# Emitting the magnitude, clamp and low word of the next weight piece one step earlier in the float64 conversion of a fused attention and expert kernel

## The chip, the cores and the metric

One NeuronCore of a Trainium2 chip runs the whole program. The metric is the device time of one execution in microseconds (us). Five engines work side by side, each through its own queue in order: TensorE (PE; PEld is its weight load), VectorE (DVE), ScalarE (ACT), GpSimd (POOL) and SyncE (SP), which issues most DMAs.

## The reference, cut to what matters

Decayed linear attention over 4 batches, 8 heads, 768 positions of 64 values gives x (3072 by 512). A capacity router gives each of 8 experts 384 tokens, and each expert applies a two-layer network to its tokens. All tokens then pass through a shared second network:

```python
    for e in range(E):
        mask = assigned == e
        h = np.maximum(x[mask] @ w1[e], 0.0)
        out[mask] = h @ w2[e]
...
    h = x @ w_in
    g = np.maximum(h, 0.0) + np.log1p(np.exp(-np.abs(h)))
    return (g @ w_out).astype(np.float32)
```

The two weights w_in (512 by 2048) and w_out (2048 by 512) reach the chip as 64-bit floats, and the kernel turns them into 32-bit floats itself.

## The kernel before, in words

**Stages.** Attention runs over 24 chunks of 128 rows (class `Attn`). The first phase of the router picks expert and tokens for the first network (class `Route`). Then the experts run one after the other (class `Ffn`), while the router's next phase is issued piece by piece between their groups of matmuls. Every fp32 product is made of three matmuls: each operand is split into a rounded high part and the rest (`whi` and `wlo`, `gh` and `gl`, `xh` and `xl`, `x2h` and `x2l`), and high times high, low times high and high times low are added up in PSUM.

**The conversion** (class `Conv`, lines 240 to 318). A piece is a tile `raw` with two 32-bit words per weight. `load` (L254) brings it by a DMA on SP. `size` (L266 to L273) makes three instructions: ScalarE takes the magnitude of the high word (Abs, L270, into `cA`), GpSimd clamps it from below in place (the maximum, L271), and ScalarE scales the low word (L272, into `cB`). Then VectorE merges the sign into `cB` (the merge, L285), VectorE shifts `cA` (the shift, L287), and GpSimd adds `cA` and `cB` (the addition, L288). In the conversion of w_in a rounded copy on ScalarE (L298) and its rest on VectorE (L293, L301) follow.

`run` is a generator and each `yield` ends one step. A piece has two steps when it has one target (w_out), and mostly three when it has two (w_in). `size` is called for a later piece, `lead` pieces ahead.

The class is used twice:

- w_in: 16 pieces of 128 by 512 during attention, `lead` 2, five buffers of `cA` and four of `cB`. Its steps are spread over the 72 places that `Attn.emit` offers by `side(j, part)`, from the tenth place on.
- w_out: 32 pieces of 128 by 256 during the first router phase and expert 0 (the late conversion), `lead` 1, three buffers of `raw` and `cA`, two of `cB`. The buffers are taken in turn, so `cB` of piece q is the buffer of piece q-2, which the addition of piece q-2 reads.

**The order of expert 0.** `Ffn.plan` writes out a list of groups of matmuls, and `Ffn.emit` goes through it. For each group it first splits the weights that will be needed some groups later (`weights`, L661 on ScalarE and L662 on VectorE), then issues the group, then the conversion's steps, then a part of the router:

```python
            self.weights(at[n] + 4)
            fn(i, f)
            if i == 0 and n > 3:
                for _ in range(1 + n % 2):
                    self.late.step()
            step += 1
            if self.listed <= i + 1 or step % 2 == 0:
                self.route()
```

So an even group takes one step and an odd group two, until the pieces are done. The first groups of expert 0 are its own network (`m1`, L684 to L687 with h1h and h1l; `m2`, L676 to L678). From n = 18 on a group of w_in (`f1`, matmuls at L684 to L687, even n) and a group of w_out (`f2`, L782 to L787, odd n) alternate, until groups that transpose expert 1's rows (`xt`, L708, with xh and xl at L671 and L672) come between. In a w_in group ScalarE makes `gh` of the group before (L761) and three activations `sp` (L744 to L746), VectorE makes `gl` (L762) and `gf` (L748). `gh` and `gl` of group f are used by the w_out group f, which comes behind the w_in group f+2.

The router's operations on VectorE that matter here are `thr` (L476), `ind` (L487), `tb` (L540) and the one-hot `ohq` (L567). Their small matmuls on TensorE (L436, L490, L543, L580) stand between the large groups. The tokens' rows of expert 1 are gathered by three DMAs on GpSimd's queue (L697).

Of the kernel before, what the change touches and what calls it, by code (L numbers as in the profile page):

```python
# [244 lines left out]
class Conv:  # L245
# [29 lines left out]
    def run(self):  # L275
        nc, v, N = self.nc, self.nc.vector, len(self.plan)
        self.ahead(0)
        ready = [self.size(q) for q in range(self.lead)]
        late = None
        for p in range(N):  # L280
            self.ahead(p + 1)
            A, B, w1 = ready.pop(0)
            to = self.plan[p][1]
            F = to[0].bitcast(I32) if len(to) == 1 else A
            v.scalar_tensor_tensor(B, w1, UPPER, B, op0=OP.bitwise_and, op1=OP.bitwise_or)  # L285
            yield
            v.tensor_scalar(A, A, 3, 0x3fffffff, op0=OP.logical_shift_left, op1=OP.bitwise_and)  # L287
            nc.gpsimd.tensor_tensor(F, A, B, op=OP.add)  # L288
            if p + self.lead < N:
                ready.append(self.size(p + self.lead))  # L290
            yield
            if late:
                v.tensor_tensor(late[1][1], late[0], late[1][0].bitcast(FT), op=OP.subtract)  # L293
                yield
            late = None
            if len(to) == 2:
                late = F.bitcast(FT).rearrange("p (a n) -> p a n", a=4), to
                nc.scalar.activation(to[0], late[0], AF.Copy)  # L298
            self.made += 1
        if late:  # L300
            v.tensor_tensor(late[1][1], late[0], late[1][0].bitcast(FT), op=OP.subtract)  # L301
        while True:
            yield self
# [703 lines left out]
```

## Time and profile before

| | |
|---|---|
| median of 3 runs | 1018.38 us (1016.86 to 1020.95) |
| profiled execution | 1018.63 us, of which the span of instructions is 1016.9 us |
| mean granted TensorE clock over the span | 0.99 |
| TensorE (PE) busy | 994.5 us, 98% |
| VectorE (DVE) busy | 637.5 us, 63% |
| ScalarE (ACT) busy | 579.9 us, 57% |
| GpSimd (POOL) busy | 160.2 us, 16% |
| loads of w_in pieces, of w_out pieces, issue to landing | 8.7 us, 3.0 us (median) |

Attention ends at about 110 us, the first router phase at about 145 us, and the late conversion's last addition starts at 252 us. A busy TensorE is not TensorE at its peak, since the ends of pipelined matmuls are modelled. A wait is put down to the instruction that released it last. Averages over the whole span say little here: the conversion lives in the first quarter.

### The profile page before, as it was taken

How to read it: one execution, taken by the hardware profiler on the slowest of the kernel's cores; microseconds unless marked ns; L12 is line 12 of the kernel's file. 1: busy time of each engine (PE TensorE's matmuls, PEld its weight loads, DVE VectorE, ACT ScalarE, POOL GpSimd, SP SyncE). 2: the span in 40 equal slices, each digit the busy share in tenths (PEclk: the TensorE clock that was granted, in tenths of full speed). 3: DMA queues.
4: the chain of work that ended last, by engine and by line, in shares of the span. 5: the costliest groups of instructions: out<-in, count | busy, mean ns of one | idle time of the engine just before them, and what ended most of it. 6: DMA issues, size and time to landing. Idle time of an engine off the chain costs nothing.

```text
span 1016.9 us, 19118 instructions
## 1 busy us (share of the span) xinstructions
PE 994.5 (98%) x7319; PEld 899.3 (88%) x7319; DVE 637.5 (63%) x1620; ACT 579.9 (57%) x1250; POOL 160.2 (16%) x185
## 2 busy tenths in 40 slices
PE   9999889999999999999999999999999999999997
PEld 8888669887998889998998899899989999999996
DVE  6989678879666656755575566555665644444442
ACT  5999425777446653665456635654366536653663
POOL 1655223556101010100110010001010010000001
PEclk9999789999999999999999999999999999999999
DMA  9998234224412023200410031103210250013000
GB/s 367 414 415 357 95 115 159 87 71 121 119 39 63 2 68 100 61 1 25 143 57 7 22 125 53 32 11 105 63 32 4 80 166 1 1 57 111 1 1 31
DMA packets 40603, 96.05 MB, mean 94 GB/s; under 512 B 5312, under 2 KB 5568, under 8 KB 40512
## 3 DMA queue, kind: packets, MB, share of 16 engines
q1 hardware_dynamic: 36528, 82.16, 23.9%
q0 software_dynamic: 3840, 12.59, 3.7%
q8 instruction: 57, 0.93, 0.4%
q14 instruction: 34, 0.28, 0.1%
q10 hardware_dynamic: 144, 0.09, 0.0%
HBM read 82.23 MB, written 12.58 MB: 93 GB/s over the span
## 4 chain that ended last, share of the span: by engine, by line
PE 75%; issue 12%; POOL 4%; DVE 4%; ACT 3%; DMA 1%; another core or an unknown queue 0%; POOLq 0%; ACTq 0%
PE h L684 11%; PE h L687 11%; PE h L685 10%; PE acc L782 7%; PE acc L783 7%; PE acc L787 7%; PE acc L676 3%; PE acc L678 3%; PE acc L677 3%; PE pA L130 2%; PE pY L158 2%; PE pX L183 2%; PE rt L436 2%; POOL wol L288 1%; POOL cA L271 1%
## 5 line engine op out<-in xcount | busy, mean ns | idle before, releaser
L748 DVE SCALAR_TENSOR_TENSOR gf<-h,sp 128x384 f32<-128x384 f32 x128 | 71.2, 556 | 186.7 <-ACT sp L746 186.7
L684 PE MATMUL h<-x2h,wih 128*128 128x384 f32 x512 | 175.6, 343 | 1.5 <-DVE xl L672 1.5
L685 PE MATMUL h<-x2h,wil 128*128 128x384 f32 x512 | 172.5, 337 | 0.0
L782 PE MATMUL acc<-whi,gh 128*128 128x512 f32 x384 | 153.3, 399 | 0.0
L783 PE MATMUL acc<-wlo,gh 128*128 128x512 f32 x384 | 151.3, 394 | 0.0
L744 ACT ACTIVATE sp<-h 128x384 f32<-128x384 f32 x128 | 62.4, 487 | 135.6 <-PE h L687 125.3
L668 ACT ACTIVATE h1h<-h 128x384 fp32r<-128x384 f32 x64 | 31.4, 491 | 147.2 <-PE h L687 105.1
L687 PE MATMUL h<-x2l,wih 128*128 128x384 f32 x512 | 112.2, 339 | 0.9 <-DVE x2l L672 0.8
L787 PE MATMUL acc<-whi,gl 128*128 128x512 f32 x384 | 111.2, 396 | 0.8 <-DVE gl L762 0.8
L795 POOL DMA_INDIRECT out_dram<-rows,ix x24 | 24.2, 1007 | 500.0 <-ACT rows L793 496.6
L684 PEld LDWEIGHTS h<-x2h,wih 128*128 128x128 f32 x512 | 96.2, 188 | 5.2 <-DVE xl L672 1.8
L685 PEld LDWEIGHTS h<-x2h,wil 128*128 128x128 f32 x512 | 96.2, 188 | 3.4
L687 PEld LDWEIGHTS h<-x2l,wih 128*128 128x128 f32 x512 | 91.3, 188 | 3.1 <-DVE x2l L672 3.1
L662 DVE TENSOR_TENSOR wlo<-wraw,whi 128x512 fp32r<-128x512 f32 x128 | 86.6, 691 | 6.5 <-ACT whi L661 6.4
L662 DVE TENSOR_TENSOR wlo<-wol,whi 128x512 fp32r<-128x512 f32 x128 | 88.9, 698 | 0.9 <-ACT whi L661 0.9
L684 PE MATMUL h<-xh,whi 128*128 128x384 f32 x256 | 88.2, 345 | 0.7 <-ACT xh L671 0.7
L787 PEld LDWEIGHTS acc<-whi,gl 128*128 128x128 f32 x384 | 72.0, 188 | 18.6 <-DVE gl L762 1.4
L676 PE MATMUL acc<-h1h,whi 128*128 128x384 f32 x256 | 88.4, 345 | 0.0
L661 ACT ACTIVATE whi<-wraw 128x512 fp32r<-128x512 f32 x128 | 76.6, 624 | 17.3 <-DMA wraw<-in_moe_w_dram 16.0
L678 PE MATMUL acc<-h1l,whi 128*128 128x384 f32 x256 | 86.1, 336 | 0.0
L685 PE MATMUL h<-xh,wlo 128*128 128x384 f32 x256 | 86.1, 336 | 0.0
L677 PE MATMUL acc<-h1h,wlo 128*128 128x384 f32 x256 | 86.1, 336 | 0.0
(199 smaller groups left out, 1902.7 us busy)
## 6 DMA issues: line engine op xcount, KB each, us to landing
wraw<-in_moe_w_dram SPq DMA_DIRECT2D x128, 256.0 KB, 2.6
qk_t<-in_qk_dram SPq DMA_DIRECT2D x24, 512.0 KB, 8.6
kv_t<-in_kv_dram SPq DMA_DIRECT2D x24, 512.0 KB, 9.0
raw<-in_moe_w_in_dram SPq DMA_DIRECT2D x16, 512.0 KB, 8.7
raw<-in_moe_w_out_dram SPq DMA_DIRECT2D x32, 256.0 KB, 3.0
xd<-xs SPq DMA_DIRECT2D x24, 256.0 KB, 4.9
rows<-xd,ix POOLq DMA_INDIRECT x24
out_dram<-rows,ix POOLq DMA_INDIRECT x24
```

The lines of the kernel that those rows point to most:

```text
L661: nc.scalar.activation(hi, raw, AF.Copy)
L662: nc.vector.tensor_tensor(lo, raw, hi.bitcast(FT), op=OP.subtract)
L676: nc.tensor.matmul(ps, wh, ah, start=start, stop=False)
L677: nc.tensor.matmul(ps, wl, ah, start=False, stop=False)
L678: nc.tensor.matmul(ps, wh, al, start=False, stop=stop)
L684: mm(ps, wh(d), ah[:, d], start=d == 0, stop=False)
L685: mm(ps, wl(d), ah[:, d], start=False, stop=False)
L687: mm(ps, wh(d), al[:, d], start=False, stop=d == 3)
L748: nc.vector.scalar_tensor_tensor(g, ps, 0.0, a, op0=OP.max, op1=OP.add)
L782: nc.tensor.matmul(ps, gh[:, s], wh, start=f == 0, stop=False)
L783: nc.tensor.matmul(ps, gh[:, s], wl, start=False, stop=False)
L787: nc.tensor.matmul(ps, gl[:, s], wh, start=False, stop=f == 15)
```

## The change

In `Conv.run`, the call of `size` for the piece `lead` ahead moves from the end of a piece's second step to the end of its first step. In program order it stood behind the shift and the addition of the present piece; now it stands ahead of them and behind the merge.

```diff
             v.scalar_tensor_tensor(B, w1, UPPER, B, op0=OP.bitwise_and, op1=OP.bitwise_or)
+            if p + self.lead < N:
+                ready.append(self.size(p + self.lead))
             yield
             v.tensor_scalar(A, A, 3, 0x3fffffff, op0=OP.logical_shift_left, op1=OP.bitwise_and)
             nc.gpsimd.tensor_tensor(F, A, B, op=OP.add)
-            if p + self.lead < N:
-                ready.append(self.size(p + self.lead))
             yield
```

Both conversions are changed by it, since both are this class.

## Rows read from the trace of the kernel before

**Rows 1.** Busy time by stage: us, PE, PEld, DVE, ACT, POOL, PEclk, DMA, GB/s
```profile
22.00:44.00 22.00, 21.62 (x342) 18.50 (x344) 18.44 (x40) 21.90 (x67) 15.27 (x10) 1.00 1.03 415
147.00:185.00 38.00, 37.13 (x295) 35.76 (x295) 30.07 (x77) 20.31 (x45) 13.92 (x15) 1.00 0.43 132
185.00:253.00 68.00, 63.52 (x389) 55.84 (x388) 57.88 (x158) 50.20 (x114) 40.50 (x44) 1.00 0.31 94
```

**Rows 2.** Waits of PE from 145 to 255 us: total us, times, longest
```profile
PE h L684 <- DVE xl L672: 1.5, 1, 1.5
PE rt L490 <- DVE ind L487: 1.4, 1, 1.4
...
PE acc L787 <- DVE gl L762: 0.8, 1, 0.8
PE rt L543 <- DVE tb L540: 0.8, 1, 0.8
```

**Rows 3.** Waits of DVE from 145 to 255 us
```profile
DVE cA L287 <- POOL cA L271: 7.4, 8, 1.4
```

**Rows 4.** Timeline of POOL, the late conversion's additions: start us, us, instruction, idle before
```profile
193.48 0.84 POOL L288 TENSOR_TENSOR wol<-cA,cB 128x256 int32<-128x256 int32 x1 [4.70 <-DVE cA L287]
...
196.13 0.74 POOL L288 TENSOR_TENSOR wol<-cA,cB 128x256 int32<-128x256 int32 x1 [0.68 <-DVE ksat L493]
...
201.23 0.84 POOL L288 TENSOR_TENSOR wol<-cA,cB 128x256 int32<-128x256 int32 x1 [0.73 <-DVE cA L287]
...
205.88 0.84 POOL L288 TENSOR_TENSOR wol<-cA,cB 128x256 int32<-128x256 int32 x1 [2.99 <-DVE cA L287]
...
211.87 0.85 POOL L288 TENSOR_TENSOR wol<-cA,cB 128x256 int32<-128x256 int32 x1 [2.38 <-DVE cA L287]
...
223.71 1.92 POOL L288 TENSOR_TENSOR wol<-cA,cB 128x256 int32<-128x256 int32 x1 [5.33 <-DVE cA L287]
...
231.96 0.85 POOL L288 TENSOR_TENSOR wol<-cA,cB 128x256 int32<-128x256 int32 x1 [1.05 <-DVE cA L287]
...
242.57 0.83 POOL L288 TENSOR_TENSOR wol<-cA,cB 128x256 int32<-128x256 int32 x1 [0.64 <-ACT whi L661]
```

**Rows 5.** Timeline of ACT, low words of the late conversion
```profile
192.84 0.41 ACT L272 ACTIVATE cB<-raw 128x256 int32<-128x256 uint32 x1
...
200.17 0.43 ACT L272 ACTIVATE cB<-raw 128x256 int32<-128x256 uint32 x1
...
206.75 0.43 ACT L272 ACTIVATE cB<-raw 128x256 int32<-128x256 uint32 x1 [0.77 <-POOL wol L288]
...
209.84 0.42 ACT L272 ACTIVATE cB<-raw 128x256 int32<-128x256 uint32 x1
...
219.11 0.42 ACT L272 ACTIVATE cB<-raw 128x256 int32<-128x256 uint32 x1
...
230.82 0.41 ACT L272 ACTIVATE cB<-raw 128x256 int32<-128x256 uint32 x1
...
241.59 0.42 ACT L272 ACTIVATE cB<-raw 128x256 int32<-128x256 uint32 x1
```

**Rows 6.** Waits of ACT from 194 to 243 us
```profile
ACT cB L272 <- POOL wol L288: 8.0, 6, 3.0
ACT sp L744 <- PE h L687: 2.3, 2, 1.9
ACT gh L761 <- DVE gf L748: 1.7, 1, 1.7
ACT cA L270 <- DMA raw<-in_moe_w_out_dram: 1.0, 2, 0.8
ACT sp L744 <- PE rt L537: 0.6, 1, 0.6
```

**Rows 7.** Timeline of DVE, the router's thresholds
```profile
196.15 0.77 DVE L476 SCALAR_TENSOR_TENSOR thr<-ksat,jio 128x32 f16<-128x32 f32 x1
...
261.97 0.21 DVE L476 SCALAR_TENSOR_TENSOR thr<-ksat,jio 128x46 f16<-128x46 f32 x1
```

## The prediction

> **What bounds the kernel now.** I read the stages first, then the waits of each engine in the stage where the change can act, then the single instructions there. TensorE is busy nearly the whole span (the table above), so a change off TensorE is worth only what it takes from, or adds to, TensorE's idle time. [Rows 1] give the three stages in which the conversion runs: in attention ScalarE is as full as TensorE (21.90 of 22 us, DMA share 1.03); in the first matmuls of expert 0 (147 to 185 us) TensorE has 37.13 of 38 us; in the long stage after it (185 to 253 us) TensorE has 63.52 of 68 us, so 4.5 us are open there, and VectorE (57.88) and ScalarE (50.20) are both loaded. [Rows 2] name what TensorE waits for: xl 1.5, ind 1.4, gl 0.8 and tb 0.8 us, each made by VectorE in its queue's order. That queue in turn waits 7.4 us in 8 places for the conversion's maximum on GpSimd [rows 3]. So the end is set by TensorE, and in this stage by a ring of ScalarE, VectorE and GpSimd that is nearly as slow.
>
> **What moves.** Per piece three instructions are issued one step earlier: Abs on ScalarE, maximum on GpSimd, low word on ScalarE. Nothing is added or removed; no DMA moves, because the loads are issued at the head of each piece as before, and SP's queue keeps its order. On GpSimd maximum p+1 now stands ahead of addition p. On VectorE nothing changes place.
>
> What matters is a reuse, not the order itself. In the late conversion cB has two buffers, so the low word of piece q may be written only when addition q-2 has read its buffer. Before, low word p+1 stood two steps behind addition p-1; now it stands one step behind. Expert 0's groups take one step (a w_in group, L684 to L687) and two steps (a w_out group, L782 to L787) in turn, so three pieces make a period of four groups. I call the w_out group that holds the second step of p and the first of p+1 **split**, and the one that holds both steps of p+2 **whole**.
>
> **Whole groups.** Before, ScalarE runs two pieces back to back behind the three sp activations and stops at the second low word until the addition of the group before: it starts at 206.75 [rows 5], when the addition of 205.88 ends [rows 4]. After, one of the two has gone forward, but the other stops for the same addition, at the same instant. Cost 0. VectorE gains: maximum p+2 is long done when the shift asks for it, so most of the 7.4 us go.
>
> **Split groups.** Before, one piece, no wait. After, that piece stands in the w_in group ahead, and the next follows at once: Abs runs, then the low word waits for addition p, which stands behind gf, the merge, routing work and the shift of this same group on VectorE. Behind that low word are queued, on ScalarE, the next whi, gh and sp, and for these wait wlo, gl, gf and the routing chain on VectorE. From the rows: the low word of 200.17 ends at 200.60 and frees ScalarE; after the change a low word of 0.43 us follows the end of the addition of 201.23, 202.07, and ScalarE is free at 202.50: 1.9 us later. In the same way, low word against addition [rows 4, 5]: 192.84 against 193.48 1.5 us, 209.84 against 211.87 2.9, 219.11 against 223.71 6.5, 230.82 against 231.96 2.0, 241.59 against 242.57 1.8. Of the 6.5 I take 4.5: that addition lasted 1.92 us where 0.84 is usual, and VectorE should come to its shift about a microsecond earlier. Sum 14.6 us.
>
> **What takes it up.** ScalarE's own idle time between them: for TensorE 2.3 and 0.6, for gf 1.7, for a load 1.0 [rows 6], and 3.0, the longest wait for an addition in [rows 6], held there by the gather of rows on GpSimd and not by the conversion's order. That is 8.6 us, which leaves 6.0. VectorE's saved waits shorten the split group of 209.84 by one wait, 1.4 us at the most [rows 3]: 4.6 us.
>
> **The port.** An operation of VectorE that meets one of GpSimd ends with it: thr takes 0.77 us from 196.15 [rows 7], and the addition of 196.13 lasts 0.74 [rows 4]; the same line takes 0.21 us at 261.97 with GpSimd free [rows 7]. After the change maximum p+1 starts just ahead of each split group, while the merge of p is due on VectorE, and addition p hangs on the shift behind that merge. It costs between nothing (the merge comes first) and a whole operation of GpSimd, 0.84 us as an addition [rows 4]. I take 0.3 in each of six places, nearer the low end, because the maximum must itself wait for Abs while gf and the merge are already next in VectorE's queue: 1.8 us. The Trainium skill ("SBUF — State Buffer", section "SBUF: two separate sides") states the rule: the pair of ports that VectorE and GpSimd share is an exclusive lock, and "the other fully blocks". The trace agrees (0.77 against 0.21 us). By the rule alone each of the six would pay the whole operation; that is a rival below.
>
> **Sum.** 4.6 and 1.8 make 6.4 us by which ScalarE is late at the end of the stage. TensorE pays it only where it has no reserve: at ind, tb, gl and xl it waits already [rows 2], and the last of them, xl, comes behind all six places; between them gh is made about two groups ahead of its use. I take two thirds, 4.3 us. Ends: nothing if the reserve takes it all, 8 us if none does and the port costs more; below nothing, the waits of TensorE that hang on VectorE alone, xl 1.5, gl 0.8 and tb 0.8, could go, minus 3.1.
>
> **Costed at nothing.** Attention: cB has four buffers there and the addition asked for is three steps back, so no new wait. The first step now holds three pieces' activations instead of two ahead of sb and vh, but ScalarE is full from 22 to 44 us [rows 1] and does the same work by the end of that stretch; bounds 1.2 us (one piece) either way. Loads: each waits for a merge that keeps its place, but Abs asks for it one step earlier; ScalarE waits 1.0 us in two places for loads now [rows 6], and where the load is later still, the low word behind it waits for its addition anyway, so I add nothing (at most another 1.0). Routing ahead of expert 0: the shifts and additions keep their order on VectorE, and GpSimd waits for them. First matmuls of expert 0: ScalarE is busy 20.31 of 38 us [rows 1], which covers the same waits; without that cover they would cost about as much as three split groups, some 5 us.
>
> The profiled execution took 1018.63 us, the median of the runs is 1018.38. 1018.63 and 4.3 make 1022.9; against the median I say 1022.7.
>
> **Rivals.** (a) *As forecast*, +2 to +7, likeliest 1022.7. For it: [rows 4, 5] fix each wait. Chance 0.45. (b) *The port decides*: the merge or shift waits a whole 0.84 us in each split group, 0.54 us more six times, 3.2: about 1025.9. It decides if Abs ends well ahead of gf in most groups. Against it: ScalarE finishes sp, for which gf waits, just ahead of Abs, so gf starts while Abs runs. Chance 0.20. The skill's rule of the exclusive lock, named above, speaks for this one. (c) *Hidden*: gh and wlo stand far enough ahead, TensorE waits as before: 1018.4. For it: ScalarE waits 8.0 us for additions already [rows 6], and TensorE's four waits come to 4.5 us [rows 2]. Chance 0.25. (d) *Faster*: the 7.4 us that VectorE waits for the maximum [rows 3] were what made xl, gl and tb late. Without them TensorE gains up to 3.1 us: 1015.3. It decides if those three waits shrink while the low words wait no longer than 8 us in that window; against it, xl needs xh, which stands on ScalarE behind the low word. Chance 0.10.
>
> **How the numbers follow.** 0.5% (5.1 us) is about what a measurement of this kernel can tell from no change. Slower by more: four tenths of (a) and nearly all of (b), 0.38. Faster by more: a corner of (d), 0.05. The rest, 0.57, is within. The range takes in (c) and most of (b), and reaches into (d): 1016.0 to 1028.5; the likeliest case alone is 1020 to 1025.5.
>
> **What would show it.** Right: the waits of the low word for the addition grow from 8.0 to over 14 us in this stage; VectorE's waits for the maximum fall under 2 us; TensorE's busy time from 185 to 253 us falls further behind, with longer waits at ind, tb, gl or xl. Wrong: the low word's waits stay near 8 us (my reading of the reuse fails), or they grow and TensorE's waits don't (case c), or the stage from 22 to 110 us changes by over 1.5 us (attention costed wrongly).

## The result and the profile after

The changed kernel takes 1029.19 us (median of 5 runs, 1028.42 to 1030.19) against 1019.28 us for the kernel before (5 runs, 1016.86 to 1020.95): ratio 1.0099, 95% interval 1.0081 to 1.0116. It is slower by 9.9 us. The sign is as forecast; the size is more than twice the 4.3 us, and the time lies just above the range (1028.5). The profiled execution took 1029.19 us with a span of 1027.4 us, 10.5 us above the span of before, so the two traces hold the whole difference.

TensorE issues the same matmuls in the same order in both, so I lay the start of the same matmul side by side and see where the lateness grows:

| TensorE's matmul | before | after | later by |
|---|---|---|---|
| third chunk of attention, L183 | 21.00 | 20.86 | -0.14 |
| fifth chunk, L183 | 29.72 | 30.52 | +0.80 |
| seventh chunk, L183 | 38.25 | 39.90 | +1.65 |
| last chunk, L183 | 110.90 | 113.55 | +2.65 |
| end of the first matmuls of expert 0, L436 | 182.36 | 185.27 | +2.91 |
| second L436 behind it | 198.15 | 202.71 | +4.56 |
| router, L543 | 214.86 | 221.41 | +6.55 |
| router, L580 | 223.38 | 231.50 | +8.12 |
| expert 1's rows, L708 | 248.96 | 258.32 | +9.36 |
| router, L436 | 255.71 | 266.07 | +10.36 |

Behind that it stays at 10.4 to 10.6. So attention lost 2.8 us, the first router phase 0.3, the first matmuls of expert 0 nothing, and the groups that share expert 0 with the late conversion 7.4 (10.36 less 2.91).

The stage windows of the changed kernel, columns as in [rows 1]:

```profile
22.00:44.00 22.00, 21.21 (x321) 17.39 (x320) 17.23 (x35) 20.43 (x59) 13.20 (x10) 1.00 1.03 415
147.00:185.00 38.00, 36.11 (x270) 34.16 (x269) 30.18 (x78) 18.66 (x40) 11.74 (x14) 1.00 0.48 145
185.00:253.00 68.00, 60.18 (x382) 52.54 (x380) 53.04 (x140) 44.35 (x102) 34.86 (x41) 0.97 0.29 88
```

Two things to see against [rows 1]; the windows are the same times, not quite the same work, since the changed kernel is already late in them. In attention ScalarE is no longer full: 20.43 of 22 us instead of 21.90. In the long stage every engine is busy for less of the 68 us, TensorE 60.18 instead of 63.52: nobody has more work, everybody waits more. And the granted clock there is 0.97 instead of 1.00.

TensorE's waits from 145 to 265 us in the changed kernel (us in total, times, longest):

```profile
PE h L684 <- DVE xl L672: 3.7, 2, 3.1
PE rt L543 <- DVE tb L540: 2.2, 1, 2.2
PE rt L490 <- DVE ind L487: 2.0, 2, 1.6
...
PE rt L436 <- DVE G L429: 1.0, 2, 0.8
...
PE acc L787 <- DVE gl L762: 0.6, 1, 0.6
```

The places are those of [rows 2], where xl, ind, tb and gl came to 4.5 us; here they and G make 9.5. The operands of the large products (gl) are not later. It is the router's small products and the splitting of expert 1's rows that come late. The matmul that waits for xl does not use it:

```profile
254.00 0.44 PE L684 MATMUL h<-x2h,wih 128*128 128x384 f32 x1 [3.05 <-DVE xl L672]
```

It belongs to a w_in group of expert 0 and multiplies x2h. By the kernel's code what it needs is a PSUM tile `h`, of which there are three: expert 1's transposed rows stand in one until xh and xl have read it.

ScalarE's waits from 197 to 251 us, the stretch that answers to [rows 6]:

```profile
ACT cB L272 <- POOL wol L290: 15.7, 10, 2.8
ACT sp L744 <- PE h L687: 2.0, 1, 2.0
ACT cA L270 <- DMA raw<-in_moe_w_out_dram: 1.1, 2, 0.8
```

The low word's wait for the addition (L290 is the addition here, L289 the shift) grew from 8.0 us in 6 places to 15.7 in 10. The waits for TensorE and for loads are as in [rows 6]; only those for gf and for the router's matmul are gone.

VectorE's waits from 145 to 265 us:

```profile
DVE wlo L662 <- ACT whi L661: 10.1, 10, 1.6
DVE gf L748 <- ACT sp L746: 5.4, 9, 0.9
```

The wait for the maximum, 7.4 us in [rows 3], is gone from the list. In its place VectorE waits 10.1 us for whi (1.1 us from 145 to 255 us before), which stands on ScalarE right behind the low word.

One split group shows the whole chain. ScalarE in the changed kernel:

```profile
214.94 0.42 ACT L272 ACTIVATE cB<-raw 128x256 int32<-128x256 uint32 x1
216.19 0.44 ACT L270 ACTIVATE cA<-raw 128x256 f32<-128x256 f32 x1 [0.83 <-DMA raw<-in_moe_w_out_dram]
217.52 0.43 ACT L272 ACTIVATE cB<-raw 128x256 int32<-128x256 uint32 x1 [0.89 <-POOL wol L290]
217.86 0.61 ACT L661 ACTIVATE whi<-wol 128x512 fp32r<-128x512 f32 x1
```

GpSimd beside it, a maximum and the addition:

```profile
215.19 0.85 POOL L271 TENSOR_SCALAR cA<-cA 128x256 f32<-128x256 f32 x1 [1.82 <-ACT cA L270]
216.65 0.84 POOL L290 TENSOR_TENSOR wol<-cA,cB 128x256 int32<-128x256 int32 x1 [0.61 <-DVE cA L289]
```

VectorE beside it, from the merge to tb:

```profile
215.22 0.65 DVE L285 SCALAR_TENSOR_TENSOR cB<-raw,cB 128x256 int32<-128x256 int32 x1
...
216.28 0.29 DVE L289 TENSOR_SCALAR cA<-cA 128x256 int32<-128x256 int32 x1
216.48 0.42 DVE L285 SCALAR_TENSOR_TENSOR cB<-raw,cB 128x256 int32<-128x256 int32 x1
218.51 0.69 DVE L662 TENSOR_TENSOR wlo<-wol,whi 128x512 fp32r<-128x512 f32 x1 [1.61 <-ACT whi L661]
...
220.40 0.56 DVE L748 SCALAR_TENSOR_TENSOR gf<-h,sp 128x384 f32<-128x384 f32 x1 [0.73 <-ACT sp L746]
...
221.08 0.28 DVE L540 CAST tb<-rt 128x128 bf16<-128x128 f32 x1
```

And TensorE, waiting for tb:

```profile
221.41 0.18 PE L543 MATMUL rt<-mem,trii 128*128 128x50 bf16 x1 [2.24 <-DVE tb L540]
```

The shift of the group (216.28) stands on VectorE behind gf, the merge and the router's operations; its addition ends at 217.49; only then may the low word that ScalarE has issued too early run (217.52). whi, gh and the three sp follow it on ScalarE, so wlo waits 1.61 us, gf 0.73, and TensorE waits 2.24 us for tb, which stands behind gf; that wait was 0.8 before [rows 2].

Behind that wait something follows that no step of the prediction has. The same columns as in [rows 1], changed kernel:

```profile
216.00:222.00 6.00, 3.76 (x21) 2.94 (x20) 3.63 (x10) 3.55 (x8) 2.44 (x5) 0.99 0.30 87
222.00:225.00 3.00, 3.00 (x11) 3.00 (x10) 2.83 (x12) 1.39 (x3) 1.66 (x2) 0.50 0.27 87
225.00:231.00 6.00, 6.00 (x30) 5.33 (x29) 4.94 (x13) 2.79 (x7) 2.00 (x3) 0.98 0.12 44
```

From 222 to 225 us the granted clock is 0.50, that is 1.2 GHz. The w_in group there lasts 3.69 us (221.46 to 225.15), the same group of before 2.16 (214.91 to 217.07). That is 1.5 of the 7.4 us. The rest is waits: by the starts of the matmuls behind each, G cost 0.5 and 1.0 us, ind 0.2 and 0.5, tb 1.5 and xl 1.5 and 0.9 more than before, 6.1 together, less 0.2 regained at small places.

### The profile page after: what moved, and what is told of

It is laid out like the page before. It is cut to its first block, busy times and chain, and to the rows that moved or that the text cites. A ratio compares the mean times of both kernels' runs of the same rounds, so it can differ in the third digit from the quotient of the medians.

```text
span 1027.4 us, 19142 instructions
## 1 busy us (share of the span) xinstructions
PE 998.8 (97%) x7319; PEld 901.5 (88%) x7319; DVE 641.4 (62%) x1620; ACT 580.3 (56%) x1250; POOL 155.5 (15%) x185
## 4 chain that ended last, share of the span: by engine, by line
PE 73%; issue 12%; DVE 6%; ACT 4%; POOL 3%; DMA 1%; another core or an unknown queue 0%; POOLq 0%; ACTq 0%; SPq 0%; DVEq 0%
PE h L684 11%; PE h L687 11%; PE h L685 11%; PE acc L782 7%; PE acc L783 7%; PE acc L787 7%; PE acc L676 4%; PE acc L678 3%; PE acc L677 3%; PE rt L436 2%; PE pY L158 1%; ACT vh L120 1%; PE pA L130 1%; PE pA L894 1%; POOL cA L271 1%
```

## The experiments

Theory: expert 0 loses by the reuse of cB, whose two buffers make a low word that is issued a step earlier wait for an addition that stands behind this very step. Rivals: the port that VectorE and GpSimd share (the maximum ahead of the merge and the shift), or ScalarE's order alone. The third chunk starts up to 1 us earlier than in the kernel before, or 0.1 later, ahead of anything that was edited; differences inside attention are therefore counted from the third chunk's L183 (a count that has an error of its own, shown with the table below), and those of expert 0 from the L436 at 182.36.

**The conversion of w_in alone, then that of w_out alone.** `lead` is 2 for w_in and 1 for w_out:

```diff
+            if p + self.lead < N and self.lead == 2:   # w_out alone: == 1
+                ready.append(self.size(p + self.lead))
             yield
...
-            if p + self.lead < N:
+            if p + self.lead < N and self.lead == 1:   # w_out alone: == 2
```

> The change in the conversion of w_in alone. Two losses that add up: the landmarks of TensorE put 2.9 us on attention, so about 1022 us (+2.9), and expert 0 as before. If attention's loss is no loss of its own but is taken up later by the router's phase, within 1 us of before.

> The change in the conversion of w_out alone. Two losses that add up: attention as before, expert 0 about 7.5 us longer, so 1026.5 us or so. If the loss in expert 0 needs the late start from attention (another phase against the router), less than 4 us.

w_in alone took 1019.66 us against 1018.16 (ratio 1.0021, 1.0012 to 1.0030). Inside attention it lost about what the whole change lost: its last L183 is 1.95 us later, 2.7 counted from the third chunk. Part of that does not reach the end: from there to 182.36 its profile is 1.6 us shorter than before, at a higher granted clock (below).

w_out alone took 1026.62 us (1.0088, 1.0075 to 1.0102). Attention ends as before (0.00 at its last L183, though the third chunk started 1.0 us earlier), and between 182.36 and 255.71 it loses 7.5 us, as the whole change does. ScalarE's longest wait from 185 to 265 us:

```profile
ACT cB L272 <- POOL wol L290: 18.6, 12, 2.8
```

So the two losses are separate: 7.5 us by w_out in expert 0, and 2.0 to 2.7 by w_in in attention.

**w_out alone, with a third buffer for cB.** To make room in SBUF the router's `tin` is put in the place of `lm`; it computes the same.

```diff
-        tin = T([128, N, E], FT, "tin")
+        tin = self.lm
...
-    F.late, F.kept = Conv(tc, ctx, 256, halves, 3), kept
+    F.late, F.kept = Conv(tc, ctx, 256, halves, 3, 1, (3, 3)), kept
```

> As e2, with three cB buffers, so that the low word waits for an addition one piece further back. Reuse theory: ScalarE's waits for the addition fall from about 21 us between 185 and 262 us to under 3, and the time is that of the kernel before or up to 3 us less (VectorE's waits for the maximum are gone too). Port and order theory (the maximum stands in front of the addition and in VectorE's way): buffers don't matter, the time stays within 2 us of e2.

It took 1016.63 us (0.9984, 0.9975 to 0.9993): faster than both kernels. Expert 0, which lost 7.5, gains 2.1 (0.73 earlier at 182.36, 2.80 earlier at 255.71). ScalarE's waits from 185 to 262 us:

```profile
ACT gh L763 <- DVE gf L750: 7.0, 6, 2.5
ACT sp L746 <- PE h L689: 6.2, 5, 1.9
ACT cA L270 <- DMA raw<-in_moe_w_out_dram: 3.0, 4, 1.3
ACT cA L270 <- POOL wol L290: 1.9, 1, 1.9
```

The low word waits for nothing any more. TensorE from 145 to 262 us:

```profile
PE rt L492 <- DVE ind L489: 1.4, 1, 1.4
PE rt L545 <- DVE tb L542: 1.1, 1, 1.1
PE h L710 <- DMA rows<-xd,ix: 0.9, 1, 0.9
PE h L686 <- ACT xh L673: 0.7, 1, 0.7
```

The waits at xl (1.5) and gl (0.8) of [rows 2] are gone. The maximum stands as far ahead as in the change, so the port cannot be what costs 7.5 us, and neither can ScalarE's order alone, which is that of the change too.

**w_out alone, Abs and maximum ahead, the low word where it was** (two buffers of cB):

```diff
+                ready.append(self.size(p + self.lead))     # Abs, maximum; w_out alone, first step
...
-                ready.append(self.size(p + self.lead))
+                ready.append(self.low(*(ready.pop() if self.lead == 1 else self.size(p + self.lead))))
```

> w_out alone: Abs and the maximum ahead, the low word at its old place. Reuse theory: the low word waits as in the kernel before, VectorE's waits for the maximum go, so before or up to 3 us less. Port and order theory: the maximum is in front here too, so 4 us or more slower than before, near e2.

It took 1018.80 us (1.0009, 0.9999 to 1.0018). Expert 0 is within 0.1 us of before (+1.00 to +1.11). That settles the loss a second time: of the three instructions moved, the low word alone is dear. But the hoped-for gain is missing, although VectorE's 7.4 us of waits for the maximum are gone. ScalarE from 185 to 262 us:

```profile
ACT cB L275 <- POOL wol L293: 10.3, 7, 3.7
```

The low word still stops for an addition, and for longer: 8.7 us in this stretch before. VectorE waits 1.1 us more there for sp and 1.8 more for whi. Together that is 4.5 us, of 6.5 that VectorE waited for the maximum in this stretch before: most of what was saved comes back between these two engines.

**The old order, with three buffers of cB.** The edit is that of the third buffer alone.

> The old order in both conversions, three cB buffers in that of w_out. If the reuse of cB costs something in the old order too (ScalarE waits 8.7 us for additions from 185 to 262 us), these waits go and the time falls by 1 to 3 us, as in e3. If the gain of e3 comes from VectorE's waits for the maximum, which the new order alone removes, the time is that of before within 0.7 us.

It took 1019.36 us against 1018.85 (1.0008, 0.9994 to 1.0022). VectorE from 145 to 265 us, and then ScalarE:

```profile
DVE cA L287 <- POOL cA L271: 7.4, 8, 1.4
```

```profile
ACT gh L761 <- DVE gf L748: 11.4, 9, 2.3
```

Now the low word's waits are gone and the wait for the maximum is as before; gh waits in the low word's place (6.7 us in that stretch before). Against before the four corners read: new order and two buffers +8.5 us, old order and three buffers +0.5 (not told from none), new order and three buffers -1.5. The earlier maximum and the third buffer each remove one wait of a ring that has two. Only together do they shorten it.

**The whole change with three buffers of cB.**

> The whole change, with three cB buffers in the conversion of w_out. If the change's loss is the reuse of cB in expert 0 plus the order in attention, the parts add up: attention ends 2.5 to 3 us later as in e1, expert 0 gains about 2 us as in e3, and the time is that of before within 2 us, some 9 us under the change with two buffers. If buffers only helped because attention was left alone in e3, it stays 4 us or more above before.

It took 1018.03 us against 1018.18 (1.0004, 0.9993 to 1.0015). Expert 0 gains 2.0 us (+1.25 to -0.76), attention loses 2.8 (-0.27 to +2.49): the loss of attention is left when that of expert 0 is taken out.

**What attention loses: four variants of w_in alone.** The maximum behind the addition, Abs and low word ahead (first diff); the first piece in the old order (second); the low word behind, Abs and maximum ahead (as above, with `lead` 2); the first two of these together.

```diff
-        self.nc.gpsimd.tensor_scalar(A.bitcast(FT), A.bitcast(FT), LEAST, None, op0=OP.max)
...
+                self.clamp(ready[-1][0])      # the maximum, behind the addition
```

```diff
+            if p + self.lead < N and self.lead == 2 and p:
...
+            if p + self.lead < N and (self.lead == 1 or not p):
```

> w_in alone: Abs and low word ahead on ScalarE, the maximum behind the addition on GpSimd as in the kernel before. Theory of ScalarE's order (the pieces stand ahead of sb and vh): attention ends 2 to 3 us later than before, as in e1. Theory of GpSimd's order (the maximum delays the addition and with it wih): attention ends within 0.7 us of before.

> w_in alone, with the first piece in the old order, so that the first step holds two pieces' activations and not three. If the first burst makes the loss up to the seventh chunk (1.8 us by the landmarks) and the rest comes later: attention ends about 1 us later than before. If any piece standing one step earlier costs the same: 2 us or more.

> w_in alone: Abs and maximum ahead, low word at its old place. ScalarE's order: half of each burst stays, so attention ends 0.5 to 2 us later than before. GpSimd's order: the maximum still stands in front, so 2 to 3 us later, as in e1.

> w_in alone: the first piece in the old order and the maximum behind the addition throughout. If the first burst and GpSimd's order are both part of attention's loss, attention ends at most 1 us later than before, less than e6 and e7, and what is left arises at the seventh chunk, where a rounded copy and a piece stand ahead of vh. If only one of the two counts, it is as late as the better of e6 and e7.

Counted from the third chunk's L183, and by the last L183 alone, attention is later by:

| w_in alone | time, before | ratio | from the third chunk | last L183 |
|---|---|---|---|---|
| all three ahead | 1019.66, 1018.16 | 1.0021 | +2.7 | +1.95 |
| maximum behind | 1020.55, 1018.85 | 1.0013 (1.0000 to 1.0025) | +1.3 | +0.81 |
| first piece old | 1020.56, 1018.85 | 1.0018 (1.0006 to 1.0031) | +1.8 | +1.62 |
| low word behind | 1019.56, 1018.85 | 1.0001 (0.9988 to 1.0014) | +1.2 | +0.40 |
| maximum behind, first piece old | 1019.57, 1018.18 | 1.0016 (1.0007 to 1.0025) | +1.3 | +0.49 |
| w_in as before (w_out alone, in its three forms above) | | | +0.4 to +1.0 | -0.2 to 0.0 |

The last row is the error of the fourth column. These runs leave w_in as it was, start 0.7 to 1.0 us early, and have lost most of that lead by the seventh chunk. The last column does not count such a lead; behind each figure stands one trace.

GpSimd's timeline in the kernel before:

```profile
23.74 3.02 POOL L271 TENSOR_SCALAR cA<-cA 128x512 f32<-128x512 f32 x2 [14.26 <-ACT cA L270]
27.12 1.29 POOL L288 TENSOR_TENSOR cA<-cA,cB 128x512 int32<-128x512 int32 x1 [0.36 <-DVE cA L287]
```

And with all three ahead:

```profile
22.97 4.64 POOL L271 TENSOR_SCALAR cA<-cA 128x512 f32<-128x512 f32 x3 [13.30 <-ACT cA L270]
27.58 1.65 POOL L290 TENSOR_TENSOR cA<-cA,cB 128x512 int32<-128x512 int32 x1
```

Three maxima in a row: the third holds up the first addition to 27.58. ScalarE in the same run then waits for that addition:

```profile
29.26 0.63 ACT L300 ACTIVATE wih<-cA 128x512 fp32r<-128x512 f32 x1 [0.84 <-POOL cA L290]
```

With the maximum behind, GpSimd:

```profile
23.24 3.02 POOL L275 TENSOR_SCALAR cA<-cA 128x512 f32<-128x512 f32 x2 [13.56 <-ACT cA L270]
26.62 1.28 POOL L294 TENSOR_TENSOR cA<-cA,cB 128x512 int32<-128x512 int32 x1 [0.36 <-DVE cA L293]
```

and ScalarE:

```profile
28.54 0.63 ACT L306 ACTIVATE wih<-cA 128x512 fp32r<-128x512 f32 x1
```

Two maxima, then the addition, as in the kernel before, and wih does not wait. TensorE's fifth chunk loses 0.9 us here too (-0.51 to +0.43), but the sixth is back at -0.54. With all three ahead the lateness of the fifth stays (+0.20, then +0.17). So the three activations ahead of sb and vh cost 0.9 us once, which ScalarE makes good when it need not wait for GpSimd. In both runs the seventh chunk loses another 0.8, but there the runs with w_in as before lose 0.3 to 0.6 of their lead as well. Taking the first piece out of it removes the loss of the fifth chunk and nothing of the seventh.

Up to the sixteenth chunk the lateness goes with the maximum. L183 is later there by 1.9 us with all three ahead, 1.6 with the first piece old and 1.4 with the low word behind, where the maximum stands ahead each time; by 0.3 and 0.0 in the two runs with the maximum behind; and by -0.2 to 0.0 with w_in as before. At the seventeenth chunk both runs with the maximum behind lose 1.1 us at once, those with all three ahead or the first piece old 0.4, the one with the low word behind nothing, and part of that is regained by the end. So the maximum ahead of the addition is what makes the lateness of the first sixteen chunks. What is lost and regained behind them I could not take apart, nor how low word and maximum, of which either alone leaves less than half at the end, make +1.95 together.

None of the four expectations is borne out as it stands. With the maximum behind, and with the first piece old, the lateness lies between the two theories; with the low word behind it depends on the count; and what is left in the last run arises at the seventeenth chunk and not at the seventh. The times do not follow the columns on attention to better than a microsecond; the first router phase differs between these runs by up to 1.8 us.

## Why the prediction was right or wrong

**The reuse of cB: right, and it is the cause.** The low word's waits grew from 8.0 to 15.7 us in the window named (over 14 was asked for), those for the maximum vanished, and TensorE waits at xl, tb and ind, as said. Removing the reuse (third buffer), or only the low word's move, removes the loss.

**Split groups, 14.6 us, and what takes it up, 8.6 and 1.4: both too large, and their difference right by luck, since the errors cancel.** From the kernel before (194 to 253 us) to the changed one (197 to 262 us) the low word's waits grew from 8.7 to 18.5 us, 9.8: 7.4 at the six that now stand in split groups, and 2.4 at the six in whole groups, which the prediction had at nothing. ScalarE's other waits fell from 6.1 to 3.1. Net 6.8 us, where the prediction had 6.4 with the port. The 3.0 us wait behind the gather of rows, which I counted as taken up, is still there:

```profile
246.40 0.43 ACT L272 ACTIVATE cB<-raw 128x256 int32<-128x256 uint32 x1 [2.57 <-POOL wol L290]
```

**TensorE pays two thirds: the step that failed in expert 0.** It paid nearly all: of ScalarE's 6.8 us, 5.9 came as TensorE's waits, and 1.5 us of lower clock on top, where 4.3 us were forecast. I argued from gh, made two groups ahead, and that held (gl 0.6, against 0.8). But the router's small products hang on VectorE's last results (tb, ind, G), have no such lead, and stand in TensorE's queue between the large groups. One such place in each stretch hands on the whole lateness, and ScalarE, with no more slack than before, never gets it back. The 1.5 us of clock stand in no term.

**The port: size right, importance none.** Five merges of the late conversion that start just behind a maximum take 0.65 or 0.66 us (215.22, above) instead of the 0.42 of 216.48, so some 0.2 in a place against my 0.3. A sixth, at 221.28, meets an addition and takes 0.98; the kernel before has one such place too (214.73, 0.97). Nor does such an operation "end with" GpSimd's, as I had read from thr: the five merges end about 0.2 us before the maximum, and the sixth 0.3 us behind the addition. The Trainium skill ("SBUF — State Buffer", section "SBUF: two separate sides") makes the shared pair of ports an exclusive lock for the whole instruction, also where VectorE's operation has two inputs in SBUF, as the merge has, and GpSimd's reads SBUF, as the maximum does; by that rule alone the merge, which lies wholly inside the maximum's 215.19 to 216.04, would have had to wait for its end. The rows show that it did not: it ran beside the maximum and was 0.2 us longer. Spans on GpSimd are rough in this profile, but all five merges show the same. Here the measurement differs from the rule, and decides. With the maximum ahead in every place, two variants lose nothing in expert 0, so rival (b) falls.

**Attention costed at nothing: the second step that failed, 2.8 us.** The prediction said that over 1.5 us here would refute it. The bound of 1.2 us (one piece on ScalarE) was that of a single engine's queue. I had noted that on GpSimd the maximum now stands ahead of the addition, and priced that only in expert 0; in attention the third maximum, 1.5 us, stands ahead of the addition on which wih hangs, and ScalarE waits for it instead of catching up. Up to the sixteenth chunk that is shown by the variants; what is lost behind it stays open. The prediction called ScalarE full there and counted on that; an engine that is full has nothing to make up a wait with.

**First matmuls of expert 0 at nothing: right** (+2.91 at 161 us and at 182.36). **Routing ahead of it at nothing: right within 0.3 us. Loads at nothing: right** (1.1 us of waits against 1.0).

**Rivals (c) and (d).** (c), hidden, falls with the result. (d), faster because VectorE no longer waits for the maximum, was right on the wait and wrong on its worth by itself: with that wait gone and the low word in its old place the time is that of before (1.0009). Its condition, that the low words wait no longer, is met only with the third buffer, and then 1.5 us of the 3.1 come.

The sum with the measured terms: 7.4 in expert 0, 2.8 in attention and 0.3 in the router make 10.5 us, the difference of the spans (a start 0.14 us early and 0.2 us lost behind expert 0 about cancel); the medians say 9.9.

## What to carry to other kernels

Before issuing a producer a step earlier in an in-order queue, ask which consumer must free its output buffer, and whether that consumer now stands behind it: if so, the engine stops there with all that follows, and a further buffer has to come with the move. Where two waits lie on one ring of engines, removing one only shows the other; price them together. And when an engine is late beside a bound engine, look for the smallest operations that connect them, with no lead, as they pass on everything.

## What the runs showed of the hardware that was not expected

The granted clock fell to 0.50 (1.2 GHz) right behind TensorE's wait of 2.24 us at tb, and stayed there for about 3 us. The same wait of 2.24 us and the same fall came with w_out alone; the kernel before and the variants with waits of 1.2 us and less at this place kept 1.00. It is no rule of the length alone: the wait of 3.05 us for xl, until 254.00 in the changed kernel, was followed by a clock of 1.00.

The first router phase runs at a clock that differs between traces of kernels whose instructions are the same there. Means over 112 to 150 us, the kernel before:

```profile
112.00:150.00 38.00, 32.61 (x265) 23.68 (x265) 28.06 (x118) 8.83 (x18) 10.39 (x12) 0.78 0.36 115
```

and w_in alone:

```profile
112.00:150.00 38.00, 30.32 (x270) 22.16 (x271) 28.89 (x122) 9.31 (x19) 10.36 (x12) 0.91 0.37 118
```

From the last L183 to the first matmuls of expert 0 (110.90 to 161 us before) w_in alone took 1.6 us less than the kernel before. Over all the traces this part took from 1.8 us less (mean clock 0.91) to 1.2 us more (0.82), and in one at 0.92 the same. So the clock goes with some of the difference and not with all of it, and the difference is as large as most of the effects measured in attention. Why the clock differs was not tried.
